# First expert unsplit and taken in one tile per batch, four more experts with unsplit first products

## Chip, cores and metric

One core of one Trainium2 chip. The time is the device time of one execution, in microseconds. A change of about 1% is what a measurement of this kernel can tell from none.

## The reference, cut to what matters

Three stages on 1536 tokens (2 batches of 768), 512 features:

```
attention, 8 heads of 64, masked to keys of the same cluster       -> x[b, s, 512]
for b, s in order:                       # 8 experts, 512 -> 1024 -> 512
    fresh = argmax(x[b,s] @ w_gate)
    e = fresh if s == 0 or sigmoid(x[b,s] @ w_local) < 0.5 else prev_e;  prev_e = e
    p = softmax(x[b,s] @ w_gate)[e]
    out[b,s] = p * (relu(x[b,s] @ w1[e]) @ w2[e])
y = (sigmoid(causal 5-tap conv of out) * (out @ w_val)) @ w_out
```

Each token goes to one expert, which is known only after its batch's attention: the choice is carried along the sequence. Counted from the reference on the inputs it draws (seed 0), the experts 0 to 7 get 54, 88, 118, 164, 82, 73, 71, 118 tokens of batch 0 and 88, 65, 62, 6, 81, 155, 140, 171 of batch 1.

## The kernel before

**Order.** The instructions of each engine stand in the order in which the program writes them, and each engine and DMA queue works its list in that order. Attention runs as 96 items (`for i in range(NI)`, lines 783 to 834); work for later stages is hung on chosen values of `i`. Routing (`route_steps`, lines 496 to 607) is done for half a batch at a time. Its fourth part needs the last item, and so stands alone between the stages: this stretch is the routing gap here. A token's row is scattered to a slot of its expert in `xslots` (`scatter`, line 611, on the POOL queue), and an expert reads its rows from there.

**Experts.** Positions `k` = 0 to 7 take experts in an order given by `AT` (0: expert 0, 1: expert 3, 6: expert 2, 7: expert 1; the four others by their counts). `CAPS` is the number of slots at each position. `HALVED` names experts with one tile for each batch; here experts 1 and 2, 128 slots each. Tokens beyond the slots go to an overflow loop after the last first products (lines 1170 to 1214), which is skipped if there are none. `do_mm1` (line 1045) makes the first products of an expert, 8 groups of 128 hidden features, with the tokens as columns; `do_mm2` (line 1119) the second, with 512 columns. Order: mm1(0), mm1(1), mm2(0), mm1(2), mm2(1), ..., mm1(7), then the halves of positions 6 and 7 (`do_half`, line 1137).

**Precision.** Operands are split in a high part in fp32r and the rest: `w_split` (line 331) copies a weight tile's half to `whi` on ACT and subtracts on DVE to `wlo`. Each product is three fp32r matmuls (line 1063 for the first products, lines 1100 to 1102 for the second). If the last tile of an expert has at most 64 rows, high and rest of its hidden values stand in one stationary operand (`FOLD`, lines 1095 to 1099) and two matmuls do. A weight tile is 1 MB, four to an expert; it lands in a staging buffer (three: `stg`) and is split into one of four pairs of buffers (`ring`).

**Fill-in work.** `tick` (line 967) stands after each group of products and pops one or two entries of `work` (splits, with the DMA of the next raw tile after the second half), two steps of `late` (the overflow plan), and one step, sometimes two, of `conv` (lines 237 to 290: 66 steps that turn the last stage's double-precision weights into two parts on DVE, ACT and POOL, in a buffer that the last stage then uses for its input). A tile of matmuls of fixed length (`keep_warm` and `spin4`, lines 852 to 859) runs in the routing gap, and its output is not used.

Of the kernel before, what the change touches and what calls it, by code (L numbers as in the profile page):

```python
# [8 lines left out]
F32 = mybir.dt.float32  # L9
# [13 lines left out]
CAPS = (192, 192, 300, 240, 224, 184, 256, 256)  # L23
PACK = 64
AT = {0: 0, 1: 3, E - 2: 2, E - 1: 1}
HALVED = (1, 2)
# [13 lines left out]
def routed_attention_moe_kernel(  # L40
# [27 lines left out]
    xin_p = apool("xin", 1)  # L68
    xx_p = apool("xx", 1)
# [27 lines left out]
    cd = cst.tile([128, 4, 32], F32, name="cd")  # L97
    cent_sb = cst.tile([128, 4, 64], F32, name="cent_sb")
# [28 lines left out]
    def const_iota(name, shape, pattern, base, mult=0):  # L127
        t = cst.tile(shape, F32, name=name)
# [3 lines left out]
    wts = const_iota("wts", [128, 24, NC_], [[0, 24], [-1, NC_]], NC_)  # L132
# [27 lines left out]
    wgl_sb = cst.tile([128, 4, 146], F32, name="wgl_sb")  # L160
# [23 lines left out]
    csq = cst.tile([128, 4, 64], F32, name="csq")  # L184
# [26 lines left out]
    worder = []  # L211
    for k in range(E):
        worder += [(k, 0), (k, 1)]
        if k:
            worder += [(k - 1, 2), (k - 1, 3)]
    worder += [(E - 1, 2), (E - 1, 3), (E, 0), (E, 1)]
    wpos = {k: j for j, k in enumerate(worder)}
    whd = dram.tile([2, 128, 2048], F32, name="whd")
# [89 lines left out]
    def ring(j):  # L308
        return rings[0] if j % R == 0 else rings[1]
# [3 lines left out]
    turn = dict(AT)  # L313

    def w_dma(j, q=None):
        k, i = worder[j]
        if k == E:
            W[worder[j]] = [
                p.tile([128, 2048], F32R, tag=g, name=n)
                for p, g, n in (((stg[1], "w", "whi"), (stg[2], "w", "wlo")), ((ring0, "hi", "whi"), (ring0, "lo", "wlo")))[i]  # L320
            ]
            nc.sync.dma_start(W[worder[j]][0].bitcast(F32), whd[i])
            nc.sync.dma_start(W[worder[j]][1].bitcast(F32), wld[i])
            return
        t = wraw[j] = stg[(j + 2) % len(stg)].tile([128, 2048], F32, tag="w", name="wraw")
        if k in AT:
            (q or nc.sync).dma_start(t, wq[4 * AT[k] + i])
        else:
            nc.sync.dma_start(t, wq[bass.ds(turn[k] * 4 + i, 1)].rearrange("o p f -> (o p) f"))

    def w_split(j, half, lo_eng=None):
        if worder[j][0] == E:
            return
# [7 lines left out]
        c = slice(1024 * half, 1024 * half + 1024)  # L341
        t = wraw[j]
        nc.scalar.copy(hi[:, c], t[:, c])  # L343
        (lo_eng or nc.vector).tensor_tensor(lo[:, c], t[:, c], hi[:, c].bitcast(F32), op=ALU.subtract)  # L344
# [425 lines left out]

    for grp in prep_steps(0):
        for f in grp:
            f()
# [9 lines left out]
    for i in range(NI):  # L783
# [53 lines left out]
    last_PV(2)  # L837
    for t in range(3):
        last_logits(t)
    att.close()  # L840
    stg[:] = [wstg, pool("wstg1"), pool("wstg2")]
    w_dma(2)
# [4 lines left out]
    for n, f in enumerate(route_steps(3)):  # L847
        if n == 1:
            last_rows()
        f()  # L850
# [3 lines left out]
    for w in (128, 192, 224, 256):  # L854
        for _ in range(8):
            nc.tensor.matmul(spin4[:, :w], onesr[:, :128], onesr[:, :w], start=True, stop=True)
    for w in (128, 192, 288):
        for _ in range(6):
            nc.tensor.matmul(spin4[:, :w], onesr[:, :128], onesr[:, w:2 * w] if w < 256 else onesr[:, :w], start=True, stop=True)


# [23 lines left out]
    def overflow_steps():  # L885
# [13 lines left out]
            lambda: [v.memset(cape[:, e:e + 1], float(128 if e in HALVED else CAPS[k])) for k, e in AT.items()],  # L899
            lambda: v.memset(cape[:, E:], 128.0),  # L900
# [36 lines left out]

    aps.close()


    xs_p = mpool("xs", 1)
    xt_p = mpool("xt", 1)
    h_p = mpool("hp", 1)
    y_p = mpool("yp", 3)
    mps = ExitStack()
    qpool = lambda name, bufs=1: mps.enter_context(tc.tile_pool(name=name, bufs=bufs, space=PSUM))
# [5 lines left out]
    def queue_w(j):  # L952
        j += R
        if j > LAST:
            return
        work.append(lambda: w_split(j, 0))
        work.append(lambda: (w_split(j, 1), w_next(j)))

    def w_next(j, q=None):
        if j + len(stg) <= LAST:  # L960
            w_dma(j + len(stg), q)
# [21 lines left out]
    FOLD = [0 < (c - 1) % 128 < PACK and n > 1 for c, n in zip(CAPS, NT)]  # L983
# [3 lines left out]
    WX = (max(CAPS[0::2]), max(CAPS[1::2]))  # L987

    XS = {}

    def load_x(k):
# [3 lines left out]
        XS[k] = xs_p.tile([128, -(-WX[k % 2] // 128), XC], F32, tag=f"xs{k % 2}", name="xs")  # L995
        if AT.get(k) in HALVED:
            for t, c in enumerate((AT[k], E + HALVED.index(AT[k]))):
                nc.sync.dma_start(XS[k][:, t, :], xslots[c * SLOT:c * SLOT + 128, :])
# [11 lines left out]
    def do_x(k, part=0):  # L1010
# [6 lines left out]
        if part == 0:  # L1017
# [4 lines left out]
            for ts, r in same:  # L1022
# [3 lines left out]
                xt_p.tile([128, 4, WX[k % 2]], F32R, tag=f"x{s}{k % 2}", name=f"x{s}") for s in ("hi", "lo")  # L1026
            ]
        hi, lo = XT[k]
# [9 lines left out]
        for a, c in qs:  # L1038
            nc.scalar.copy(hi[:, c, :w], xp[:, a, :w])  # L1039
        for a, c in qs:  # L1040
# [439 lines left out]
```

## Time and profile before

| | |
|---|---|
| median of 3 runs (lowest, highest) | 548.25 us (547.82, 551.88) |
| the profiled execution, and its span | 548.82 us, 547.1 us |
| busy share of the span: PE, DVE, ACT, POOL | 96%, 72%, 61%, 20% |
| attention and three parts of routing | to 262 us |
| routing gap | 262 to 280 us |
| experts | 280 to 470 us |
| last stage | 470 to 547 us |

A busy PE is not PE at its peak: matmuls are pipelined, so what a matmul costs is read from the distance between starts, not from its duration. An fp32 matmul shows as two records, an fp32r one as one.

### The profile page before, as it was taken

The numbers are of one execution on the slowest core, as the hardware profiler recorded it, in microseconds if no ns is written. First come the engines' busy times: TensorE is split into PE (matmuls) and PEld (weight loads), VectorE is DVE, ScalarE is ACT, GpSimd is POOL, SyncE is SP. The second block draws the span as 40 slices with busy tenths as digits, with TensorE's granted clock in tenths as the row PEclk, the third lists the DMA queues.
The fourth block names the chain that finished last, engine by engine and source line by source line (L and its number), as shares of the span: only waits on it lengthen the run. The fifth ranks groups of instructions, "written<-read, shape, count | busy, mean of one in ns | idle before, by whom it ended". The sixth has DMA issues, their size and how long they took to land. (4 is left out here: it accounts for less than half of the span.)

```text
span 547.1 us, 9226 instructions
## 1 busy us (share of the span) xinstructions
PE 525.0 (96%) x3361; PEld 421.3 (77%) x3362; DVE 395.2 (72%) x720; ACT 334.6 (61%) x616; POOL 110.8 (20%) x109
## 2 busy tenths in 40 slices
PE   7898999999999999999799999999999999999996
PEld 3675767777677767767489798889889888899885
DVE  5585757575677867645727999979896993499970
ACT  3596868677777778675224665547465664285642
POOL 5011002020204030030400051444535244100000
PEclk9899999999999999999799999999999999999999
DMA  6867697878786757401747867787977677550023
GB/s 141 224 136 227 140 282 193 242 225 225 248 209 222 159 204 155 140 12 68 243 165 272 284 230 242 248 298 236 298 274 263 214 280 256 185 220 1 21 96 115
DMA packets 35205, 107.96 MB, mean 197 GB/s; under 512 B 4753, under 2 KB 5265, under 8 KB 30548
## 3 DMA queue, kind: packets, MB, share of 16 engines
q1 hardware_dynamic: 31700, 98.35, 59.0%
q0 software_dynamic: 2496, 8.40, 4.0%
q10 hardware_dynamic: 960, 0.58, 0.3%
q8 instruction: 27, 0.44, 0.3%
q14 instruction: 22, 0.18, 0.1%
HBM read 58.57 MB, written 29.13 MB: 160 GB/s over the span
## 5 line engine op out<-in xcount | busy, mean ns | idle before, releaser
L653 DVE TENSOR_REDUCE mx<-s 128x1 f32<-128x768 f32 x96 | 91.6, 955 | 59.3 <-PE s L646 51.5
L682 ACT COPY pt<-tp 128x384 f32<-128x384 f32 x148 | 65.7, 484 | 55.1 <-PE tp L677 55.0
L662 ACT ACTIVATE pexp<-s,mx 128x768 f32<-128x768 f32 x96 | 87.2, 908 | 6.6 <-DVE mx L653 4.6
L344 DVE TENSOR_TENSOR wlo<-wraw,whi 128x1024 fp32r<-128x1024 f32 x62 | 84.7, 1381 | 3.8 <-ACT whi L343 3.7
L677 PE MATMUL tp<-ident,pexp 128*128 128x128 f32 x576 | 81.2, 277 | 0.3 <-DVE pt L680 0.2
L677 PEld LDWEIGHTS tp<-ident,pexp 128*128 128x128 f32 x576 | 68.2, 142 | 7.7 <-ACT pt L682 3.4
L343 ACT CAST whi<-wraw 128x1024 fp32r<-128x1024 f32 x64 | 64.9, 1045 | 10.3 <-DMA wraw<-in_wq_dram 10.3
L689 PE MATMUL pv<-pt,vt 128*64 128x384 f32 x360 | 67.8, 498 | 0.1
L642 PE MATMUL s<-st 128*128 128x384 f32 x188 | 57.4, 387 | 1.5 <-ACT pexp L662 1.5
L646 PE MATMUL s<-st 80*128 80x384 f32 x188 | 48.9, 341 | 1.4 <-DMA st<-ohr 1.4
L1101 PE MATMUL yp<-wlo,h 128*128 128x512 f32 (+3 forms) x104 | 41.4, 398 | 1.6 <-DVE wlo L344 1.1
L642 PEld LDWEIGHTS s<-st 128*128 128x128 f32 x188 | 28.6, 191 | 18.4 <-issue 6.7
L1100 PE MATMUL yp<-whi,h 128*128 128x512 f32 (+3 forms) x104 | 41.1, 395 | 0.8 <-PEq L1170 0.8
L1071 ACT ACTIVATE h<-hps 128x384 fp32r<-128x384 f32 (+5 forms) x36 | 18.5, 514 | 38.2 <-PE hps L1066 38.1
L1066 PE MATMUL hps<-xhi,whi 128*128 128x192 f32 (+5 forms) x256 | 41.1, 282 | 0.6 <-ACT xhi L1039 0.6
L1102 PE MATMUL yp<-whi,h 128*128 128x512 f32 (+3 forms) x104 | 41.0, 394 | 0.0
L689 PEld LDWEIGHTS pv<-pt,vt 128*64 128x64 f32 x360 | 21.9, 136 | 24.1 <-issue 23.7
L1066 PE MATMUL hps<-xlo,whi 128*128 128x192 f32 (+5 forms) x256 | 40.4, 279 | 0.0
L1066 PE MATMUL hps<-xhi,wlo 128*128 128x192 f32 (+5 forms) x256 | 40.3, 280 | 0.0
L362 POOL TENSOR_TENSOR xx<-xkq,xx 128x768 fp32r<-128x768 f32 x8 | 14.6, 1819 | 117.9 <-ACT xx L356 117.9
L1066 PEld LDWEIGHTS hps<-xhi,whi 128*128 128x128 f32 x256 | 34.9, 190 | 1.7 <-ACT xhi L1039 0.8
L646 PEld LDWEIGHTS s<-st 80*128 80x128 f32 x188 | 34.5, 190 | 1.7 <-issue 1.7
(269 smaller groups left out, 953.2 us busy)
## 6 DMA issues: line engine op xcount, KB each, us to landing
wraw<-in_wq_dram SPq DMA_DIRECT2D x30, 1024.0 KB, 7.1
st<-xx SPq DMA_DIRECT2D x48, 384.0 KB, 6.1
xslots<-padrow SPq DMA_DIRECT2D x14, 771.0 KB, 11.0
xkq<-in_kq_dram SPq DMA_DIRECT2D x15, 384.0 KB, 5.1
wspace<-in_wd_dram SPq DMA_DIRECT2D x8, 512.0 KB, 6.2
xall<-xnat SPq DMA_DIRECT2D x4, 771.0 KB
vt<-in_v_dram SPq DMA_DIRECT2D x8, 384.0 KB, 3.4
out_dram<-os SPq DMA_DIRECT2D x11, 256.0 KB, 2.0
```

The lines of the kernel that those rows point to most:

```text
L343: nc.scalar.copy(hi[:, c], t[:, c])
L344: (lo_eng or nc.vector).tensor_tensor(lo[:, c], t[:, c], hi[:, c].bitcast(F32), op=ALU.subtract)
L642: nc.tensor.matmul(ps[:, n, :384], st[:, 1, q0:q0 + 128], st[:, 0, 384 * n:384 * n + 384], start=True, stop=False)
L646: nc.tensor.matmul(ps[:, n, :384], st[0:80, 2, q0:q0 + 128], st[0:80, 3, 384 * n:384 * n + 384], start=False, stop=True)
L653: nc.vector.tensor_reduce(mx, ps[:, :, :384], axis=AX.XY, op=ALU.max, negate=True)
L662: nc.scalar.activation(pt, ps[:, :, :384], AF.Exp, bias=mx[:, 0:1], accum_out=Zt[i // 6][:, t, h:h + 1])
L677: nc.tensor.transpose(tp[:, k, :], p[:, 128 * kt:128 * kt + 128], ident)
L682: nc.scalar.copy(dst, tp)
L689: nc.tensor.matmul(PVs[u][64 * h:64 * h + 64, :], Vt[g][:, kt, h, :], PT[u, h][:, kt, :], start=(kt == 0), stop=(kt == NQT - 1), skip_grou ...
L1066: nc.tensor.matmul(hp, a[:, d, fs], c[:, d, :w], start=(n + d == 0), stop=(n + d == 5))
L1100: nc.tensor.matmul(yp[:r], h[:, fa, hi], whv[:, f, :], start=(q == 0 and f == 0), stop=False)
L1101: nc.tensor.matmul(yp[:r], h[:, fa, hi], wlv[:, f, :], start=False, stop=False)
```

## The change

Expert 0 has a tile for each batch now (`HALVED` = 0, 1, 2), 128 slots each, so there are 11 slot ranges in place of 10. Its weights stay fp32 and unsplit, in all four tiles, and so do its tokens and hidden values: one fp32 matmul in place of three fp32r ones. The tile of batch 0 is read in item 84 (`early_load`), transposed in item 89 (`early_rows`), and its first products are placed between the steps of the fourth part of routing, where the unused matmuls were; its second products follow, with the transposes of batch 1's tile before the last one. Then mm1(0), mm2(0), mm1(1), mm1(2), mm2(1) and so on.

Positions 1, 5, 6, 7 take unsplit fp32 first products (`WHOLE`); their second products stay split. Slots: position 1 192 to 176, 5 184 to 176, 6 and 7 256 to 192 (expert 2 as 128 and 64, which is folded; expert 1 as 96 and 96). An unsplit tile goes by DMA straight to its ring buffer once the tile before it there is used; the staging buffers hold only split tiles, in order of need (`pending`). The ring slot that shares `ring0` is now the last of four.

```diff
-CAPS = (192, 192, 300, 240, 224, 184, 256, 256)
+CAPS = (128, 176, 300, 240, 224, 176, 192, 192)
+WHOLE = (0, 1, 5, 6, 7)
-HALVED = (1, 2)
+HALVED = (0, 1, 2)
+ROWS = {0: (128, 128), 1: (96, 96), 2: (128, 64)}
...
+    def early_load():
+        EA["xs"] = xin_p.tile([128, 2, S], F32, tag="x", name="exs")[:, 0, :XC]
+        nc.sync.dma_start(EA["xs"], xslots[0:128, :])
...
+        for d in range(4):
+            nc.tensor.transpose(xp[:, 128 * d:128 * d + 128], xs[:, 128 * d:128 * d + 128], ident)
+        EA["x"] = xx_p.tile([128, 4, S], F32, tag="xx", name="exx")[:, 0, :512]
+        nc.scalar.copy(EA["x"], xp)
...
         if i == 82:
-            w_dma(0)
-        if i in (84, 88):
-            w_split(0, (i - 84) // 4, nc.gpsimd)
+            w_whole(0, ring0)
+        if i == 86:
+            w_whole(1, ring0, "lo")
         if i == 90:
-            w_dma(1)
+            w_whole(2, wstg, "w")
+        if i == 84:
+            early_load()
+        if i == 89:
+            early_rows()
...
-    w_dma(2)
+    w_whole(3, stg[1], "w")
...
-    keep_warm(ps_t.tile([128, 512], F32, tag="t", name="spin3"), 10)
-    spin4 = ps_t.tile([128, 512], F32, tag="t", name="spin4")
...
+    def early_products():
+        x = EA["x"].rearrange("p (d c) -> p d c", d=4)
+        for q in range(2):
+            wv = W[0, q].rearrange("p (d f) -> p d f", d=4)
+            for f in range(4):
+                for d in range(4):
+                    yield nc.tensor.matmul(
+                        eh[:, q, 128 * f:128 * f + 128], wv[:, d, 128 * f:128 * f + 128], x[:, d, :],
+                        start=(d == 0), stop=(d == 3), skip_group_check=True,
+                    )
...
+    r1()
+    last_rows()
+    early(9)
+    r2p()
+    r2d()
+    r3()
+    early(6)
+    r3p()
+    r4()
+    early(3)
+    r4p()
+    r4d()
+    r5()
+    early(32)
+    for q in range(2):
+        for c in range(2):
+            early_relu(q, c)
...
+        if k in WHOLE:
+            (a, c), (a2, c2) = qs
             nc.scalar.copy(hi[:, c, :w], xp[:, a, :w])
+            nc.vector.tensor_copy(hi[:, c2, :w], xp[:, a2, :w])
...
+            if k in WHOLE:
+                terms = [(W[k, q].rearrange("p (d f) -> p d f", d=4), xs[0])]
+            else:
+                whv, wlv = [t.rearrange("p (d f) -> p d f", d=4) for t in W[k, q]]
+                terms = [(whv, xs[0]), (whv, xs[1]), (wlv, xs[0])]
...
+            if k == 0:
+                nc.tensor.matmul(yp[:r], h[:, fa, hi], whv[:, f, :], start=(q == 0 and f == 0), stop=(q == 1 and f == 3))
+                continue
...
     load_x(0)
     load_x(1)
+    w_whole(R, ring1)
+    w_whole(R + 1, ring1)
     for n, k in enumerate(free):
         turn[k] = nc.sync.value_load(ordi[0:1, n:n + 1], min_val=NF, max_val=E - 1)
-    nc.gpsimd.tensor_copy(gate[:TR[1][1], 2:3], XS[1][:TR[1][1], 1, 513:514])
-    w_dma(3, nc.gpsimd)
-    w_split(1, 0)
-    w_split(1, 1)
-    w_next(1, nc.gpsimd)
-    for j in range(2, R):
-        work.append(lambda j=j: w_split(j, 0))
-        work.append(lambda j=j: (w_split(j, 1), w_next(j)))
-    do_x(0)
-    work.insert(2, lambda: keep_rows(3))
+    w_stage(stg[2])
+    queue_split(R + 2)
+    ey = ps_y.tile([128, 512], F32, tag="y", name="ey")
+    for q in range(2):
+        wv = mm2_weights(0, q)[0]
+        for f in range(4):
+            fa = 4 * q + f
+            if fa == 7:
+                do_x(0)
+            nc.tensor.matmul(ey, ehh[:, fa, :], wv[:, f, :], start=(fa == 0), stop=(fa == 7))
+    y = y_p.tile([128, 512], F32, tag="y", name="ysb")
+    nc.scalar.activation(y, ey, AF.Copy, scale=EA["pw"])
+    scatter(x2d, EA["ids"], y, 2 * S, "rows of different tokens")
+    work += [lambda: None, lambda: None, lambda: keep_rows(3)]
     late += overflow_steps()
     do_mm1(0)
     XS["ready"] = True
-    for k in range(1, E - 1):
+    do_mm2(0)
+    do_mm1(1)
+    for k in range(2, E - 1):
         do_mm1(k)
         do_mm2(k - 1)
```

## Rows read from the trace of the kernel before

**Rows 1.** Windows: start:end, length; busy time and (instructions) of PE, PEld, DVE, ACT, POOL; clock; DMA share; GB/s.
```profile
280.41:305.96 25.55, 24.76 (x213) 23.78 (x213) 17.23 (x54) 11.37 (x18) 1.34 (x3) 1.00 0.77 272
305.96:329.32 23.36, 23.36 (x147) 21.61 (x145) 23.12 (x48) 14.91 (x23) 7.08 (x5) 1.00 0.69 238
...
445.73:470.57 24.84, 23.22 (x102) 18.42 (x101) 10.84 (x14) 9.85 (x14) 7.70 (x6) 1.00 0.70 235
```

**Rows 2.** Waits of PE after 262 us: what waited, for what, total, times, longest.
```profile
PE yp L1101 <- DVE wlo L344: 1.1, 2, 0.7
...
PE xp L1034 <- DVE xlo L1041: 0.8, 1, 0.8
```

**Rows 3.** Timeline of PE, routing gap: start, length, line, work, count, [idle before].
```profile
261.85 1.01 PE L754 MATMUL po<-wgl_sb,ut 128*128 128x146 f32 x6
264.82 0.49 PE L530 MATMUL rps<-ident,rr 128*1 128x128 f32 x3 [1.96 <-DVE rr L521]
266.58 0.48 PE L542 MATMUL rps<-ident,sc 1*128 1x1 f32 x3 [1.27 <-DVE sc L534]
...
267.72 4.43 PE L112 MATMUL spin<-onesb 128*128 128x512 bf16 x10
...
278.78 1.02 PE L1034 MATMUL xp<-ident,xs 128*128 128x128 f32 x8 [0.56 <-DMA xs<-xslots]
280.41 0.85 PE L1066 MATMUL hps<-xhi,whi 128*128 128x192 f32 x4 [0.61 <-ACT xhi L1039]
```

**Rows 4.** Timeline of the SP queue: the first experts' token rows are asked for.
```profile
275.72 2.10 SPq L1006 DMA_DIRECT2D xs<-xslots  x4
```

**Rows 5.** Timeline of PE in attention: the only fp32 products with 128 stationary columns.
```profile
222.97 1.01 PE L714 MATMUL po<-wgl_sb,ut 128*128 128x146 f32 x6
223.72 0.61 PE L642 MATMUL s<-st 128*128 128x384 f32 x2
...
251.82 0.91 PE L714 MATMUL po<-wgl_sb,ut 128*128 128x146 f32 x6
252.66 1.53 PE L739 MATMUL pv<-pt,vt 128*64 128x128 f32 x24
```

**Rows 6.** Timeline of PE among the experts: split products in fp32r, three widths.
```profile
282.16 0.61 PE L1066 MATMUL hps<-xhi,whi 128*128 128x192 f32 x4
282.61 0.61 PE L1066 MATMUL hps<-xhi,wlo 128*128 128x192 f32 x4
...
436.13 0.64 PE L1066 MATMUL hps<-xlo,whi 128*128 128x256 f32 x4
436.61 0.63 PE L1066 MATMUL hps<-xhi,wlo 128*128 128x256 f32 x4
...
451.62 0.40 PE L1101 MATMUL yp<-wlo,h 128*128 128x512 f32 x1
451.85 0.39 PE L1102 MATMUL yp<-whi,h 128*128 128x512 f32 x1
```

**Rows 7.** Costliest groups of the page: the high half of a weight split on ACT.
```profile
L343 ACT CAST whi<-wraw 128x1024 fp32r<-128x1024 f32 x64 | 64.9, 1045 | 10.3 <-DMA wraw<-in_wq_dram 10.3
```

**Rows 8.** Windows, columns as in Rows 1: two weight tiles in flight.
```profile
284.00:290.00 6.00, 6.00 (x55) 5.77 (x55) 4.75 (x19) 3.40 (x6) 0.00 (x0) 1.00 0.79 330
```

**Rows 9.** Timeline of POOL, end of the experts: conversion, then the first halves' scatters.
```profile
455.61 2.15 POOL L265 TENSOR_TENSOR wspace<-wspace 128x512 f32<-128x512 f32 x1 [10.44 <-ACT wspace L261]
...
460.54 1.03 POOL L613 DMA_INDIRECT x2d<-ysb,ids  x1 [0.16 <-issue]
```

**Rows 10.** Chain that ended last, end of the experts: start, length, what.
```profile
461.87 4.07 DMA x2d<-ysb,ids
...
466.38 4.15 DMA x2nat<-x2d
```

**Rows 11.** Windows, columns as in Rows 1: the clock in the routing gap.
```profile
262.00:268.00 6.00, 2.47 (x21) 1.73 (x22) 4.29 (x21) 2.51 (x5) 2.40 (x3) 0.82 0.98 298
268.00:274.00 6.00, 6.00 (x26) 3.61 (x25) 4.38 (x17) 0.00 (x0) 2.94 (x3) 0.61 0.61 238
```

More of the change, by code (lines that the diff above doesn't have):

```diff
@@ L208, in routed_attention_moe_kernel @@
     nc.vector.tensor_copy(xnat[:, :, 513], tokid)
[L211 to L215, printed above, removed]
+    worder = [(0, 0), (0, 1), (0, 2), (0, 3), (1, 0), (1, 1)]
+    for k in range(2, E):
+        worder += [(k, 0), (k, 1), (k - 1, 2), (k - 1, 3)]
     worder += [(E - 1, 2), (E - 1, 3), (E, 0), (E, 1)]
     wpos = {k: j for j, k in enumerate(worder)}
+    whole = [k == 0 or k in WHOLE and i < 2 for k, i in worder]
     whd = dram.tile([2, 128, 2048], F32, name="whd")
@@ L846, in routed_attention_moe_kernel, with early, early_relu @@
     rings[1] = ring1
[L847 to L850, printed above, removed]
-    keep_warm(ps_t.tile([128, 512], F32, tag="t", name="spin3"), 10)
-    spin4 = ps_t.tile([128, 512], F32, tag="t", name="spin4")
[L854 to L859, printed above, removed]
+    h_p = mpool("hp", 1)
+    WX = (max(CAPS[0::2]), max(CAPS[1::2]))
+    ehh = h_p.tile([128, 8, 2 * WX[1]], F32, tag="h1", name="ehh")[:, :, :128]
+    def early_products():
[8 more added lines that the diff above has]
+                    )
+    ep = early_products()
+    def early(n):
+        for _ in range(n):
+            next(ep, None)
+    def early_relu(q, c):
+        hp = eh[:, q, 256 * c:256 * c + 256].rearrange("p (f n) -> p f n", f=2)
+        nc.scalar.activation(ehh[:, 4 * q + 2 * c:4 * q + 2 * c + 2], hp, AF.Relu)
+    r1, r2p, r2d, r3, r3p, r4, r4p, r4d, r5 = route_steps(3)
+    r1()
[15 more added lines that the diff above has]
+            early_relu(q, c)
     lt_p = mpool("lt", 1)
@@ L955, in queue_w, with queue_split @@
             return
+        if whole[j]:
+            w_whole(j, ring(j))
+        else:
+            queue_split(j)
+    def queue_split(j):
         work.append(lambda: w_split(j, 0))
[L957 to L961, printed above, removed]
+        work.append(lambda: (w_split(j, 1), w_stage(home[j])))
     conv = convert_steps(wide.tile([128, 12, XC], F32, tag="xn", name="wspace"))
@@ L982, in routed_attention_moe_kernel @@
     NT = [-(-c // 128) for c in CAPS]
-    FOLD = [0 < (c - 1) % 128 < PACK and n > 1 for c, n in zip(CAPS, NT)]
+    FOLD = [
+        ROWS[AT[k]][1] == PACK if k and AT.get(k) in HALVED else 0 < (c - 1) % 128 < PACK and n > 1
+        for k, (c, n) in enumerate(zip(CAPS, NT))
+    ]
     TR = [
@@ L1025, in do_x @@
             XT[k] = [
-                xt_p.tile([128, 4, WX[k % 2]], F32R, tag=f"x{s}{k % 2}", name=f"x{s}") for s in ("hi", "lo")
+                xt_p.tile([128, 4, WX[k % 2]], F32 if k in WHOLE else F32R, tag=f"x{s}{k % 2}", name=f"x{s}")
+                for s in ("hi", "lo")[:1 if k in WHOLE else 2]
             ]
-        hi, lo = XT[k]
+        hi = XT[k][0]
         xp = ps_x.tile([128, 1024], F32, tag="x", name="xp").rearrange("p (d c) -> p d c", d=4 // parts)
@@ L1062, in do_mm1 @@
                     hp = hps[fi][:, 0, :w] if w > 256 else hps[0][:, fi, :w]
-                    terms = [(whv, xhi), (whv, xlo), (wlv, xhi)]
-                    for n, (a, c) in enumerate(terms if k else terms[::2] + terms[1:2]):
+                    for n, (a, c) in enumerate(terms):
                         for d in range(4):
-                            nc.tensor.matmul(hp, a[:, d, fs], c[:, d, :w], start=(n + d == 0), stop=(n + d == 5))
+                            nc.tensor.matmul(
+                                hp, a[:, d, fs], c[:, d, :w], start=(n + d == 0), stop=(n + d == len(terms) + 2)
+                            )
                 m = 2 // len(hps)
@@ L1115, in mm2_weights @@
     def mm2_weights(k, q):
-        whi, wlo = W[k, 2 + q]
-        return whi.rearrange("p (f d) -> p f d", f=4), wlo.rearrange("p (f d) -> p f d", f=4)
+        parts = W[k, 2 + q] if k else [W[0, 2 + q]] * 2
+        return [t.rearrange("p (f d) -> p f d", f=4) for t in parts]
     def do_mm2(k):
@@ L1131, in do_mm2 @@
                     tick()
-            queue_w(wpos[k, 2 + q])
+            if k:
+                queue_w(wpos[k, 2 + q])
+            else:
+                w_stage(stg[q])
         HT.pop(k)
```

125 lines of the change are left out of this document (78 added, 47 removed).

## The prediction, made before the changed kernel was run

> **What bounds the kernel now.** I read the windows by stage first. Among the experts PE is busy 24.76 of 25.55 us in the first stretch and all of the second [rows 1]; the waits of PE there are small [rows 2]. So the matmul stream sets the time of this stage, and a change is worth what it takes out of that stream, where the other engines keep up. DVE is the one to fear: 23.12 of 23.36 us in the second stretch [rows 1]. Then the timeline of the routing gap: PE has nothing that matters between the last logits at 261.85 and the transposes at 278.78; at 267.72 the unused matmuls begin [rows 3]. What ends the gap is the chain routing, scatter, load: the rows are asked for at 275.72 [rows 4]. So work that is put into the gap is free as long as it delays neither the routing steps nor the first transposes. Last the end of the experts: the last stage starts when the first halves' scatter has landed and been read back [rows 10], not when PE is done: PE is busy 23.22 of 24.84 us there [rows 1].
>
> **The price of a matmul.** Split: four matmuls of 192 columns take 282.61 - 282.16 = 0.45 us, so 0.1117 each; of 256 columns 0.48, with the rounding of longer stretches 0.118; of 512 columns 0.23, 0.2315 over longer stretches [rows 6]. From 192 to 256 columns the price hardly moves. Unsplit fp32: three matmuls of 146 columns, six records, take 0.75 us to the next matmul's start in one place and 0.84 in another, 0.125 or 0.140 a record [rows 5]. At 2.4 GHz, 2 x 146 columns take 0.1217: a record streams its columns twice, plus 0.003 to 0.018. I take the middle, 0.0105, and a floor of 0.1117 for 128 columns, since even 192 split columns cost that. A record then costs 0.117 at 128 columns (0.112 to 0.125), 0.157 at 176 (0.150 to 0.165), 0.170 at 192 (0.163 to 0.178), and 0.437 at 512 (0.430 to 0.445); a product is two records. No fp32 row is wider than 146 with 128 stationary columns, so 512 is extrapolated. So unsplit against split, for one product: 0.234 against 0.335 at 128, 0.314 against 0.335 at 176, 0.340 against 0.354 (256 columns before) at 192. Only expert 0 gains much.
>
> The Trainium skill says the same in other terms: true fp32 is four passes through the array ("FP8 and Floating Point Precision", TensorE Precision Notes), and a warm pass costs its columns plus about 2.5 ns ("TensorE: Matmul & The Clock Gate", Part 1). That is an estimate of 0.223, 0.303, 0.330 and 0.863 for the four products; the terms of PE below would sum to 1.7 us less. The row at 0.84 speaks against it, the row at 0.75 for it.
>
> **The change part by part**, against the profiled 548.82 us.
>
> 1. *Attention*, +0.45 (0.3 to 1.0). Four more transposes, about 0.13 each (eight in 1.02 [rows 3], with one start-up), on a full PE. One ACT copy comes, two casts of 1.045 [rows 7] and two subtractions on POOL go; the two small DVE copies wait for a load asked for five items earlier. DMAs: three weight tiles here in place of two, at the end of attention, where nothing else is asked for; one more slot fill on SP.
>
> 2. *Routing gap*, +0.3 (0 to 1.6). Nine products, 18 x 0.117 = 2.1 us, stand ahead of the step at 264.82; from the end of the logits (three products after 261.85, 262.7) they end at 264.8. Six take 1.4, where the next pause is 1.27; three take 0.7, where it is shorter. Each delays the chain by a tenth or two. The 14 left, 3.3 us, end near 271.8 with the shift of part 1. Seven of the second products (7 x 0.87 = 6.1) end near 278, before the rows land near 279.5; the eighth covers the copies after the transposes. So mm1(0) starts near 281.1, where it was 280.41. If the relus or the fourth weight tile were late, the slack of 1.5 us pays first.
>
> 3. *Expert 0*, -5.5 (-5.9 to -4.8). Before: 96 x 0.1117 = 10.72 and, folded, 40 x 0.2315 = 9.26. Now on the path, batch 1's tile alone: 64 x 0.117 = 7.5 and 16 x 0.437 = 7.0.
>
> 4. *First products of positions 1 and 5*, -1.4 (-2.3 to -0.3): 64 x 0.157 = 10.05 for 10.72, twice.
>
> 5. *First products of 6 and 7*, -0.9 (-1.8 to +0.1): 64 x 0.170 = 10.9 for 96 x 0.118 = 11.33, twice.
>
> 6. *End of the experts*, -2.3 (-3.6 to -0.5). The second half of position 6 is folded: 16 matmuls for 24, 1.85 us. PE was busy 23.22 there, 96 x 0.2315 = 22.2 of it matmuls; 88 matmuls and the same rest are 21.4 of the 24.84 [rows 1]. But the chain decides. There are fewer ticks, and counting them the conversion's last POOL work moves behind the first scatter. POOL had it from 455.61 to 460.5, and both scatters stood behind it [rows 9]. Now, from the end of mm1(7): one half is 24 x 0.2315 = 5.6, with the rest of 1.0 and an eviction shorter than a cast the first scatter stands on POOL at 7.3 for 1.0; the conversion's 4.9 end at 13.2, the other scatter (its half is done at 12.1) at 14.3; it lands 4.07 later and is read back 4.15 later [rows 10]: 22.5. What is late next is this chain, by a microsecond over PE. That is 2.3 less than 24.84.
>
> 7. *Waits of PE between 296 and 446*, -0.5 (-1.5 to 0). Of 64 half-tile splits 24 go, so ACT loses 24 x 1.045 [rows 7] and DVE as many subtractions. The waits for `wlo` and `xlo` are 1.9 us [rows 2]; I take a quarter, as the 40 splits left come one a tick through the stretch where DVE is full.
>
> 8. *A new wait on ACT*, +0.5 (0 to +5). Position 2's first raw tile is now asked for behind the token rows and two unsplit tiles, near 278, on SP. Its split stands on ACT between the first and second relu of mm1(0). 3.75 MB at the 330 GB/s of two tiles in flight [rows 8] take 11.4 us, to 289.4. mm2(0) starts near 289.5, and wants the second relu two products later, at 291.3; cast and relu before it take about 1.5. Behind that relu stand the other cast, the copies of the next expert and two relus, all wanted later. So it fits by a few tenths, and the rate decides.
>
> Sum: 0.45 + 0.3 - 5.5 - 1.4 - 0.9 - 2.3 - 0.5 + 0.5 = -9.35, so 539.5 for the profiled execution. The median stands 0.57 lower than that one: 539.0. Ends of all terms: -14.8 and +2.1.
>
> **Rivals.**
>
> *The raw tile is late.* If three tiles and the rows move at the 272 GB/s of the whole first stretch [rows 1], they land at 292, and mm2(0) waits 2 to 3 us; with the other DMAs of this time between them, 6 to 8. Then 541.5 to 547. For it: all of this is now on one queue and ACT works in order. Against: DMA was busy 0.79 of the time at 330 GB/s, not full [rows 8]. Chance 0.13.
>
> *Unsplit first products gain nothing off expert 0.* With 0.018 a record, parts 4 and 5 give -0.2, and if DVE, full in the second stretch, takes the rest, 541.5 to 543. Chance 0.10.
>
> *Slower: the clock falls in the gap.* In the gap the granted clock was 0.82 and then 0.61 of full in two stretches of 6 us [rows 11]: at half for some 7 us, after PE had been busy 2.47 of 6 us. If it falls there now, and the fp32 products with their small pauses don't bring it back, the second early products and mm1(0) take 7 and 7.5 us more: -9.35 + 14.5 = +5, 554 and more. It decides once it lasts beyond the gap. Against: PE would now pause hardly at all, and the granted clock was full in the first stretch, with its transposes and waits [rows 1]. Chance 0.03. The Trainium skill bears on it ("TensorE: Matmul & The Clock Gate", Part 4): transposes don't count as PE activity for the clock. By that rule, the transposes before mm1(0) are a pause; the full clock that the trace shows in the first stretch, which has transposes in it, speaks for no harm.
>
> *Slower: a token too many.* The slots are now near the counts: 62 for 64 (expert 2, batch 1), 170 for 176, 163 for 176, 211 for 224. By the counts no expert overflows, before or after. If one did, the loop would load 4 MB with nothing beside it (13 us at 330 GB/s) and compute for some 15: 565 to 570. Chance 0.02.
>
> **How the numbers follow.** The forecast, 0.70: 535 to 542.8, 539.0 likeliest. The rest of the chance (0.02) is for what I have not seen. A measurement of this kernel tells about 1% from no change, so faster is below 542.8. Faster: 0.70, with 0.05 of the late tile and 0.05 of the second rival: 0.80. Same: 0.15. Slower: 0.05. The range leaves out the clock and the overflow, and the best ends all together: 534.5 to 545.5.
>
> **What would show it.** Starts of two-record products at 128 and 512 columns (parts 2, 3), mm1(0) starting within a microsecond of 281 and mm1(1) near 296, with no wait of PE at mm2(0) (part 8). Positions 1 and 5 near 10 us, 6 and 7 near 10.9. The first transposes of the last stage 22 to 23 us after the end of mm1(7), released by the read-back. Wrong: a clock below 1.00 after 280, a wait of PE for a relu at mm2(0), or an overflow loop in the trace.

## The result, and the profile after

The changed kernel takes 540.33 us (median of 5 runs, 539.74 to 541.24) against 548.25 for the kernel before (5 runs beside it, 547.82 to 551.88). The ratio is 0.9844, with a 95% interval of 0.9809 to 0.988, so it is faster by 1.2 to 1.9%. The prediction said 539.0, within 534.5 to 545.5. The number is near, but behind it two errors of about 8 us each nearly cancel: a wait that was not foreseen, and gains that were larger (2.5 us of them scatter between executions).

The profiled execution took 539.74 us (span 538.1). The two spans are 9.0 us apart. Starts on TensorE cut them into six stretches:

| stretch, by starts on PE | before | after | change | predicted |
|---|---|---|---|---|
| start to the last logits | 261.85 | 259.77 | -2.1 | +0.45 |
| to the first products of position 0 | 18.56 | 18.41 | -0.15 | +0.3 |
| to the first products of position 2 | 34.84 | 35.69 | +0.85 | -5.7 |
| to the second products of position 6 | 131.32 | 126.21 | -5.1 | -2.1 |
| to the first transposes of the last stage | 22.99 | 20.47 | -2.5 | -2.3 |
| to the end | 77.54 | 77.55 | 0 | 0 |

The fourth column is the profile's, the last is the prediction's terms put into these stretches (-0.7 of part 4 in each of the two expert stretches). The third stretch is the miss: the first products of positions 0 and 1 and the second of 0 were to get 5.7 us shorter, and got 0.85 longer.

The timeline of PE after the change, from the gap to the last stage (columns as in [rows 3]):

```profile
260.62 2.17 PE L902 MATMUL eh<-exx,wone 128*128 128x128 f32 x18
...
266.00 3.37 PE L902 MATMUL eh<-exx,wone 128*128 128x128 f32 x28
269.92 6.28 PE L1257 MATMUL ey<-wone,ehh 128*128 128x512 f32 x14 [0.54 <-ACT ehh L915]
276.85 0.63 PE L1118 MATMUL xp<-ident,xs 128*128 128x128 f32 x4 [0.66 <-DMA xs<-xslots]
...
282.62 3.84 PE L1155 MATMUL hps<-xhi,wone 128*128 128x128 f32 x32
286.30 7.22 PE L1188 MATMUL yp<-wone,h 128*128 128x512 f32 x16
293.36 4.94 PE L1155 MATMUL hps<-xhi,wone 128*128 128x176 f32 x32
...
299.04 2.65 PE L1155 MATMUL hps<-xhi,wone 128*128 128x176 f32 x16
308.54 1.45 PE L1118 MATMUL xp<-ident,xs 128*128 128x128 f32 x6 [6.85 <-DVE xlo L1129]
309.92 4.24 PE L1155 MATMUL hps<-xhi,wone 128*128 128x176 f32 x16
...
428.71 10.56 PE L1155 MATMUL hps<-xhi,wone 128*128 128x192 f32 x64
440.08 0.47 PE L1195 MATMUL yp<-whi,h 128*128 128x512 f32 x1 [0.81 <-ACT h L1162]
...
460.55 1.47 PE L1377 MATMUL x2p<-ident,x2nat 128*128 128x128 f32 x12
```

The gap now holds expert 0's first tile, and the waits in it are a few tenths. At 308.54 stands what the prediction did not have: PE waits 6.85 us, in the middle of position 1's first products, for a transpose buffer that is free once VectorE has subtracted the low parts (`xlo`) of the tokens of position 2. Behind it sixteen records take 4.24 us, where sixteen alike took 2.65 before it. The granted clock says why (windows of the changed kernel, columns as in [rows 1]):

```profile
274.00:280.00 6.00, 5.34 (x29) 3.27 (x28) 0.64 (x3) 1.06 (x2) 0.17 (x1) 1.00 0.79 272
...
306.00:310.00 4.00, 1.46 (x7) 1.08 (x7) 4.00 (x16) 1.05 (x1) 0.00 (x0) 0.54 1.01 424
310.00:314.00 4.00, 4.00 (x17) 4.00 (x18) 2.20 (x6) 0.66 (x1) 0.00 (x0) 0.60 0.98 348
```

In the gap, where [rows 11] showed 0.82 and 0.61, the clock is now full (1.00 in the 6 us before these, too). After the long wait it is 0.54 and 0.60, that is 1.2 GHz for part of the stretch. The wait and this cost 6.85 + 1.6 = 8.4 us.

The list of PE's waits from 255 to 470 us in the changed kernel (columns as in [rows 2]) has nothing else of this size, and the waits on `wlo` are gone from it:

```profile
PE xp L1118 <- DVE xlo L1129: 6.9, 1, 6.9
...
PE yp L1195 <- ACT h L1162: 0.8, 1, 0.8
```

Why is the low part late? First VectorE's timeline in the changed kernel, then the SP queue's (start, length, line, work):

```profile
304.58 0.43 DVE L230 TENSOR_SCALAR wspace<-wspace 128x512 int32<-128x512 int32 x1 [4.14 <-DMA wspace<-in_wd_dram]
...
307.02 0.42 DVE L233 TENSOR_SCALAR wspace<-wspace 128x512 int32<-128x512 int32 x1
...
307.72 0.76 DVE L1129 TENSOR_TENSOR xlo<-xp,xhi 128x600 fp32r<-128x600 f32 x1
```

```profile
279.24 11.41 SPq L326 DMA_DIRECT2D wraw<-in_wq_dram  x2
290.94 1.69 SPq L1089 DMA_DIRECT2D xs<-xslots  x3
292.68 0.58 SPq L514 DMA_DIRECT2D xall<-xnat  x1
301.00 0.36 SPq L260 DMA_DIRECT2D wspace<-in_wd_dram  x1
```

Read from the bottom. `wspace`, the conversion's buffer, is the buffer that held the tokens' rows `xnat`, so its load at 301.00 waits until the copy asked at 292.68 is done (SP stands 7.4 us there). VectorE has the first conversion steps (lines 230 to 233) ahead of `xlo`, and stands 4.14 us at the first. In the kernel before, the copy was asked as late, at 292.60, and the load at 299.22; but there `xlo` stood ahead of the first conversion step (VectorE's timeline of the kernel before):

```profile
301.56 0.77 DVE L1041 TENSOR_TENSOR xlo<-xp,xhi 128x600 fp32r<-128x600 f32 x1
...
305.27 0.43 DVE L226 TENSOR_SCALAR wspace<-wspace 128x512 int32<-128x512 int32 x1 [0.67 <-DMA wspace<-in_wd_dram]
```

The change puts the second products of position 0, with their ticks, between the first products of positions 0 and 1, where they stood behind both. So the conversion, which starts after the first products of position 0, is popped earlier than position 2's tokens.

ScalarE's timeline has the raw tile that part 8 feared (changed kernel):

```profile
286.72 1.05 ACT L360 CAST whi<-wraw 128x1024 fp32r<-128x1024 f32 x1 [6.17 <-DMA wraw<-in_wq_dram]
287.67 0.38 ACT L1162 ACTIVATE h<-hps 128x256 f32<-128x256 f32 x1
```

The relu ends at 288.05. The second products start at 286.30 and want it with their third, four records of 0.429 later, at 288.02. It all but fits: to the next work the sixteen records take 7.06 us, against 6.87 in the kernel with the tile second (below), where it lands earlier. So the wait is 0.2 us.

The end of the experts, POOL's timeline in the changed kernel, answers to [rows 9]:

```profile
446.91 1.01 POOL L635 DMA_INDIRECT x2d<-ysb,ids  x1 [7.87 <-ACT ysb L1203]
448.98 1.29 POOL L269 TENSOR_TENSOR wspace<-wspace 128x512 f32<-128x512 f32 x1 [1.06 <-ACT wspace L265]
...
453.04 0.95 POOL L635 DMA_INDIRECT x2d<-ysb,ids  x1 [0.16 <-issue]
```

The order is the predicted one: first scatter, conversion, second scatter. The page's group for the high halves has 40 casts where [rows 7] had 64:

```profile
L360 ACT CAST whi<-wraw 128x1024 fp32r<-128x1024 f32 x40 | 40.7, 1046 | 31.8 <-DMA wraw<-in_wq_dram 16.8
```

### The profile page after: what moved, and what is told of

Read it like the earlier page. It is cut to its first block, busy times and chain, and to the rows that moved or that the text cites. A ratio compares the mean times of both kernels' runs of the same rounds, so it can differ in the third digit from the quotient of the medians.

```text
span 538.1 us, 8817 instructions
## 1 busy us (share of the span) xinstructions
PE 515.7 (96%) x3189; PEld 409.4 (76%) x3190; DVE 353.1 (66%) x693; ACT 310.0 (58%) x592; POOL 91.3 (17%) x106
## 4 chain that ended last, share of the span: by engine, by line
PE 41%; DMA 5%; SPq 1%; DVE 1%; ACT 1%; issue 1%; ACTq 0%; DVEq 0%
PE hps L1155 13%; PE yp L1195 4%; PE yp L1197 4%; PE yp L1196 4%; PE vp L1421 2%; PE vp L1427 2%; PE vp L1422 2%; PE op L1467 2%; PE op L1466 2%; PE op L1465 2%; DMA xall<-xnat 2%; PE yp L1192 1%; PE yp L1193 1%; DMA wraw<-in_wq_dram 1%; PE xp L1118 1%
## 5 line engine op out<-in xcount | busy, mean ns | idle before, releaser
L366 DVE TENSOR_TENSOR wlo<-wraw,whi 128x1024 fp32r<-128x1024 f32 x40 | 52.9, 1330 | 29.6 <-ACT whi L360 29.6
L360 ACT CAST whi<-wraw 128x1024 fp32r<-128x1024 f32 x40 | 40.7, 1046 | 31.8 <-DMA wraw<-in_wq_dram 16.8
L1155 PE MATMUL hps<-xhi,wone 128*128 128x192 f32 (+2 forms) x320 | 50.7, 318 | 0.0
L1155 PEld LDWEIGHTS hps<-xhi,wone 128*128 128x128 f32 x320 | 49.0, 195 | 1.6 <-ACT xhi L1124 0.6
L1162 ACT ACTIVATE h<-hps 128x352 fp32r<-128x352 f32 (+5 forms) x36 | 16.9, 474 | 33.8 <-PE hps L1155 33.7
L1195 PE MATMUL yp<-whi,h 128*112 128x512 f32 (+4 forms) x88 | 35.0, 397 | 0.8 <-ACT h L1162 0.8
L1197 PE MATMUL yp<-whi,h 128*112 128x512 f32 (+4 forms) x88 | 34.7, 394 | 0.0
L1196 PE MATMUL yp<-wlo,h 128*112 128x512 f32 (+4 forms) x88 | 34.7, 394 | 0.0
L1407 DVE SCALAR_TENSOR_TENSOR gt<-xf,convw_sb,gt 128x768 f32<-128x768 f32 x32 | 32.0, 1015 | 0.4
L1165 DVE SCALAR_TENSOR_TENSOR h<-hps,h 128x128 fp32r<-128x128 f32 (+7 forms) x52 | 18.4, 391 | 16.7 <-ACT h L1162 15.1
```

Source lines behind the costliest of these rows:

```text
L366: nc.vector.tensor_tensor(lo[:, c], t[:, c], hi[:, c].bitcast(F32), op=ALU.subtract)
L1155: nc.tensor.matmul(hp, a[:, d, fs], c[:, d, :w], start=(n + d == 0), stop=(n + d == len(terms) + 2))
L1195: nc.tensor.matmul(yp[:r], h[:, fa, hi], whv[:, f, :], start=(q == 0 and f == 0), stop=False)
L1196: nc.tensor.matmul(yp[:r], h[:, fa, hi], wlv[:, f, :], start=False, stop=False)
L1197: nc.tensor.matmul(yp[:r], h[:, fa, lo], whv[:, f, :], start=False, stop=(q == 1 and f == 3))
```

## The experiments

**Is it the late copy?** The first two kernels move the copy of the tokens' rows, out of the fill-in work to the queue's list in the gap: behind the load of position 2's raw tile, or ahead of it.

```diff
     w_stage(stg[2])
+    keep_rows(3)                # first kernel; the second has it ahead of w_stage
...
-    work += [lambda: None, lambda: None, lambda: keep_rows(3)]
+    work += [lambda: None] * 3
```

> The copy of the last routed rows to the overflow buffer is asked for right behind the first raw tile of position 2, before that tile's buffer blocks the SP queue, and not in the ticks of mm2(0). Theory: PE's 6.9 us wait in mm1(1) comes from the conversion's first DVE step, which waits for its load, which waits for this copy; it goes, and with it the half clock behind it: 531.5 to 533.5, no wait of PE over 1.5 us between 280 and 440, clock 1.00 there. Rival: DVE is late in mm1(1) because of the raw tiles and ACT's order; then the wait stays or moves, 539 to 541.

Measured: 537.07 us (536.31 to 538.2), ratio 0.9794 (0.9759 to 0.983). The lines of PE:

```profile
291.18 5.42 PE L1188 MATMUL yp<-wone,h 128*128 128x512 f32 x12 [1.76 <-ACT h L1162]
...
307.29 0.89 PE L1118 MATMUL xp<-ident,xs 128*128 128x128 f32 x6 [2.66 <-DVE xlo L1129]
308.12 2.65 PE L1155 MATMUL hps<-xhi,wone 128*128 128x176 f32 x16
```

The wait on `xlo` falls from 6.85 to 2.66, and the sixteen records behind it are at 2.65 again: the copy's lateness was most of it. What is left is VectorE's order, and a new wait of 1.76 on the relu, since the copy now shares the queues with the raw tile. So the expectation was too good by 3.5 us.

> As the first, but the copy stands ahead of the raw tile. Theory of the raw tile (term 8 of the prediction): 0.77 MB at about 400 GB/s push it 1.9 us later, its cast on ACT holds the second relu of mm1(0) back, and PE waits 1 to 2 us at mm2(0): 1 to 2 us slower than the first. Rival: the raw tile has more slack than that; then no wait at mm2(0) and the same time as the first within 0.5.

Measured: 540.65 us (538.95 to 542.52), ratio 0.9853 (0.9816 to 0.9891), no better than the change itself and 3.6 us slower than the first, where 1 to 2 were expected. The lines of PE:

```profile
293.31 8.43 PE L1188 MATMUL yp<-wone,h 128*128 128x512 f32 x12 [4.31 <-ACT h L1162]
...
311.45 0.89 PE L1118 MATMUL xp<-ident,xs 128*128 128x128 f32 x6 [1.68 <-DVE xlo L1129]
312.27 4.33 PE L1155 MATMUL hps<-xhi,wone 128*128 128x176 f32 x16
```

With the copy's 0.8 MB (384 rows of 2 KB) ahead of it the raw tile makes the second products wait 4.31 us, and the twelve records take 8.43 for 5.42. Behind the wait on `xlo`, here only 1.68, sixteen records take 4.33 for 2.65. The late raw tile is the mechanism of part 8 and of the first rival (a wait of 2 to 3 us, or of 6 to 8), only with a cause that the change does not have.

**Which parts carry the gain?** One kernel keeps expert 0 and position 1 unsplit, with all the new slots, and splits positions 5, 6, 7 again. The other is the kernel before with only the shorter slots of positions 1, 5, 6, 7.

```diff
-WHOLE = (0, 1, 5, 6, 7)
+WHOLE = (0, 1)
```

> The changed kernel with the first products of positions 5, 6 and 7 split again, same slots. Theory (a record costs 0.1487 at 176 and 0.1627 at 192 columns): +1.2 for position 5, +0.3 each for 6 and 7, and 0 to 1 for twelve more half-tile splits on ACT and DVE: 542 to 543.5. Rival (unsplit first products gain nothing off expert 0): 540 to 541.

Measured: 545.3 us (12 runs, 543.07 to 547.24), ratio 0.9936 (0.9909 to 0.9962): the three unsplit positions are worth about 5 us, more than expected, and against -1.6 in parts 4 and 5 for them. From the logits to the second products of position 6 the profiled execution loses 2.1 us on the change's (1.8 of it from the first products of position 2 on, what the expectation has for the records), at the end 0.7, in the last stage 1.5; another 1.2 stand ahead of the last logits, where the kernels do not differ. So half of what the splits can have cost lies outside the stream of products: with 52 half-tile splits in place of 40, a pair of them stands on VectorE at 441.34 for 5.30 us (3.09 in the change), and the conversion and the read-back are late behind it (PE waits 1.2 us for the read-back).

```diff
-CAPS = (192, 192, 300, 240, 224, 184, 256, 256)
+CAPS = (192, 176, 300, 240, 224, 176, 192, 192)
+ROWS = {1: (96, 96), 2: (128, 64)}
```

> The kernel before with the slots of the change at positions 1, 5, 6 and 7, everything split and expert 0 as before. Theory: first products of 6 and 7 from 256 to 192 columns, 0.6 us each; the folded second half of position 6, 1.85 to 3.2 at the end of the experts: 543.5 to 545.5. Rival: the chain scatter, read back sets the end and the folded half gains nothing: 546.5 to 547.5.

Measured: 550.46 us (12 runs, 544.54 to 551.8), ratio 1.0015 (0.9984 to 1.0047): no gain, where some 4 us were expected. PE and ACT show where it went:

```profile
450.25 0.59 PE L1105 MATMUL yp<-wlo,h 128*128 128x512 f32 x1 [4.77 <-issue]
```

```profile
449.47 1.99 ACT L344 CAST whi<-wraw 128x1024 fp32r<-128x1024 f32 x2 [4.49 <-DMA wraw<-in_wq_dram]
```

From the logits to the second products of position 6 it wins 2.0 us; then the last raw tile, of position 7, has not landed, PE waits 4.77 us for its halves and goes on at a lower clock (0.68 from 445 to 452, 0.81 from 452 to 458), and the end is 4.2 us longer than before. Shorter products bring PE sooner to a tile that comes no sooner. In the change, where the first products of positions 6 and 7 need no split, this wait does not appear.

**Can the rest of the wait go?** From here the copy stays early. The raw tile of position 2 is asked ahead of the slots' rows, in the queue's idle time (the numbers of the experts' tiles are read into registers ahead of it, for it needs one); in a second kernel the copy goes there too.

```diff
+    w_stage(stg[2])             # and keep_rows(3), in the second kernel
     load_x(0)
     load_x(1)
     w_whole(R, ring1)
     w_whole(R + 1, ring1)
+    keep_rows(3)                # first kernel
...
-    w_stage(stg[2])
```

> The changed kernel with the raw tile of position 2 asked ahead of the loads of the slots' rows, in the queue's idle time of the gap, and the copy of the tokens' rows right behind the loads of the gap. Theory (the queue of SP, blocked by the last raw tile, makes the copy late, the copy makes the conversion's load late, and VectorE, in order, holds the conversion's first step ahead of the tokens' low parts of position 2): the copy lands at about 286, the first products of position 1 wait at most 1.5 us on the low parts (6.85 in the changed kernel, 2.7 in the kernel with the copy right behind the tile's load), and the second products of position 0 wait on no relu; 531.5 to 534. Rival A: the early megabyte competes with the rows of the slots, the first products of position 0 start a microsecond or more later, 535 to 537. Rival B: the wait stays near 2.7 because VectorE's steps ahead of the low parts set it, not the load; 534 to 536.

Measured: 535.63 us (534.36 to 537.43), ratio 0.9764 (0.9725 to 0.9804). No wait at the second products and 1.66 on `xlo`, near the 1.5 that the theory allowed; but also the wait of its rival A, ahead of the transposes of position 0 (PE's timeline):

```profile
279.03 0.63 PE L1118 MATMUL xp<-ident,xs 128*128 128x128 f32 x4 [2.47 <-DMA xs<-xslots]
...
280.57 5.16 PE L1155 MATMUL hps<-xhi,wone 128*128 128x128 f32 x32
```

With the megabyte ahead of them PE waits 2.47 us for the 128 rows of 2 KB, for 0.66 in the change, and the 32 records behind that wait take 5.16 us for 3.74.

> As the kernel with the raw tile of position 2 in the idle time, but with the copy of the tokens' rows there too, ahead of the loads of the slots' rows. If the queue of SP alone orders these transfers, the same time within 1 us. If transfers that run together slow each other, the rows of the slots come later, and the first products of position 0 start 1 to 4 us later, 533 to 537.

Measured: 540.36 us (539.33 to 543.35), ratio 0.9861 (0.9821 to 0.99). The first entry of PE's waits:

```profile
PE xp L1118 <- DMA xs<-xslots: 6.4, 1, 6.4
```

Later than expected, too (533 to 537). With 1.8 MB ahead PE waits 6.4 us for the rows: the queue has time to spare in the gap, the DMA engines do not (their share is 1.04 from 276 to 282, for 0.79 from 274 to 280 in the change).

**Is it the order on VectorE?** Here only the start of the conversion moves behind the first products of position 1: in the change as it stands, and then in the kernel with the tile in the idle time.

```diff
     do_mm1(0)
-    XS["ready"] = True
     do_mm2(0)
     do_mm1(1)
+    XS["ready"] = True
```

> The changed kernel, in which only the conversion of the last weights begins later, behind the first products of position 1; its copy of the tokens' rows stays late. Theory (the conversion's first step stands ahead of the low parts on VectorE and waits for its load): the wait of 6.85 us goes to at most 1, and with it the stretch at the lower clock behind it; 531.5 to 534. Rival (the low parts are late for a reason of their own, the rows of position 2 or the copy to the high parts): the wait stays at 4 us or more, 538 to 540. Third: the conversion is pushed past the end of the experts and gives 1 to 4 us back there, 534 to 537.

Measured: 540.62 us (539.36 to 543.25), ratio 0.9863 (0.9824 to 0.9902): no better than the change, in sum. PE's timeline says that the theory is right and the time was given back:

```profile
302.04 0.89 PE L1118 MATMUL xp<-ident,xs 128*128 128x128 f32 x6 [0.83 <-DVE xlo L1129]
...
432.58 0.47 PE L1195 MATMUL yp<-whi,h 128*128 128x512 f32 x1 [0.82 <-ACT h L1162]
...
456.65 0.63 PE L1377 MATMUL x2p<-ident,x2nat 128*128 128x128 f32 x4 [3.46 <-DMA x2nat<-x2d]
```

The wait goes from 6.85 to 0.83 with the copy as late as in the change (asked at 292.33), so the order decides, not the copy alone: the wait needs both. (Another 0.9 us on the second `xlo` comes behind it, in the first products of position 2.) The second products of position 6 start at 432.58 for 440.08, but the last stage starts 24.1 us behind them for 20.5, and more is lost to its own waits and clock.

> As the kernel with the raw tile of position 2 in the idle time, and the conversion of the last weights begins only behind the first products of position 1. Theory: no step of the conversion is ahead of the low parts of position 2's tokens on VectorE, so the wait on them goes to at most 0.5 us; 531 to 533. Rival: the conversion then runs past the last first products and lengthens the end of the experts by 1 to 4 us, 533 to 537.

Measured: 541.01 us (539.77 to 542.27), ratio 0.9861 (0.9824 to 0.9899): no wait on `xlo` at all, 4.4 us of waits on the read-back. Its rival had the mechanism; the time is above the rival's 533 to 537 as well.

The next two let the conversion catch up, with a second step at every second or third tick where the code has every fourth (`beats[0] % 4 == 3`).

> The kernel with the later conversion, in which a second step of the conversion now goes with every second tick in place of every fourth, so that it ends about where it does in the changed kernel. Theory (the late conversion removed the wait of 6.85 us on the low parts and gave it back at the end of the experts, as 4.8 us of waits on the read-back and a half clock behind them, because the conversion's buffer is the read-back's and VectorE's and POOL's last steps stand ahead of the last scatters): the read-back's waits fall to at most 1 us, the wait on the low parts stays at most 1.5; 531 to 534. Rival (the loss at the end comes from the experts ending sooner than the read-back can, whatever the conversion does): the waits of 4 us stay, 538 to 541.

> The same with a second step at every third tick: some five steps fewer made up. If the end of the conversion decides, the waits on the read-back lie between those of the two others, 533 to 538; if it does not, the same as the kernel with the later conversion, 538 to 541.

Measured: 537.32 us (535.56 to 539.93), ratio 0.9782 (0.9749 to 0.9815), and 537.76 (536.53 to 538.61), ratio 0.9799 (0.9768 to 0.983). Both better than 540.62, so the end of the conversion does decide; neither gets under 1 us of wait on the read-back (4.5 and 2.8 in all), and the second is no worse than the first. The theory's size was off again.

**The best order.** The raw tile is asked between the rows of position 0 and those of position 1; else as in the kernel with the tile in the idle time. The second of this pair starts the conversion two ticks later.

```diff
     load_x(0)
+    w_stage(stg[2])
     load_x(1)
     w_whole(R, ring1)
     w_whole(R + 1, ring1)
+    keep_rows(3)
...
-    w_stage(stg[2])
```

> The changed kernel with the raw tile of position 2 asked between the two loads of slots' rows, ahead of the 2 MB of unsplit tiles, and the copy of the tokens' rows right behind these. Theory: the rows of position 0 are not delayed (first transposes within 0.5 us of where they stand in the changed kernel, counted from the routing's logits; 2.5 us later in the kernel with the tile ahead of all loads), the relu of position 0 waits for no raw tile, the low parts of position 2 make a wait of at most 2.7; 533 to 535.5. Rival (the megabyte delays whatever stands behind it): the rows of position 1 or the unsplit tiles of position 1 come late, a wait of 1 to 4 us ahead of the first products of position 1, 536 to 540.

Measured: 532.1 us (531.5 to 533.79), ratio 0.9698 (0.9674 to 0.9723), faster than both kernels and than the expected 533 to 535.5: its interval lies under the change's 0.9809 to 0.988. PE's timeline, then SP's:

```profile
277.33 0.63 PE L1118 MATMUL xp<-ident,xs 128*128 128x128 f32 x4
...
286.77 7.03 PE L1188 MATMUL yp<-wone,h 128*128 128x512 f32 x16
293.64 4.94 PE L1155 MATMUL hps<-xhi,wone 128*128 128x176 f32 x32
...
303.50 0.89 PE L1118 MATMUL xp<-ident,xs 128*128 128x128 f32 x6 [1.66 <-DVE xlo L1129]
...
453.34 1.47 PE L1378 MATMUL x2p<-ident,x2nat 128*128 128x128 f32 x12
```

```profile
274.56 0.34 SPq L1077 DMA_DIRECT2D xs<-xslots  x1
275.13 0.35 SPq L326 DMA_DIRECT2D wraw<-in_wq_dram  x1
...
278.11 0.38 SPq L514 DMA_DIRECT2D xall<-xnat  x1
285.03 0.35 SPq L326 DMA_DIRECT2D wraw<-in_wq_dram  x1
```

The rows of position 0 don't wait, the second products run through, and what is left of the 8.4 us is 1.66. From the first products of position 0 to those of position 2 it takes 28.03 us, for 35.69 in the change.

> The same with the conversion of the last weights beginning behind the second products of position 0, two ticks later. If VectorE's order (the conversion's first steps ahead of the low parts) sets the rest of the wait, it falls by 1 to 2 us, 532 to 534.5; if the end of the experts is then bound by the read-back, it comes back there and the time is that of the kernel before it, within 1 us.

Measured: 537.78 us (534.08 to 539.76), ratio 0.9794 (0.976 to 0.9829). The waits of PE:

```profile
PE x2p L1378 <- DMA x2nat<-x2d: 2.8, 2, 2.0
PE hps L1155 <- DVE xlo L1129: 1.7, 1, 1.7
```

The wait on the first `xlo` is gone, so VectorE's order did set it. The conversion's steps now stand ahead of the second `xlo`, for the same 1.7 us, and two ticks come back at the end: 2.1 us up to the last stage and 0.9 in it, not the one allowed for. Put together, twelve kernels with the new order show the end's rule. Both columns count from the start of position 6's second products:

| kernel | last conversion result is written out | last stage starts |
|---|---|---|
| the change; copy behind the tile; copy ahead of it; tile in the idle time; tile and copy there; tile second | 12.8 in each | 20.5 in each |
| positions 5, 6 and 7 split again | 14.9 | 21.2 |
| late, every second tick | 16.7 | 22.5 |
| late, every third tick; tile second and two ticks later | 17.3, 17.3 | 22.5, 22.6 |
| late; tile in the idle time and late | 18.9, 18.9 | 24.1, 24.1 |

The read-back lands in the conversion's buffer, and it is asked 2.4 to 3.4 us after that last write in each of them. It does not wait for a scatter there: in the kernel with two ticks later the second scatter is issued at 445.99, the last write at 450.87, the read-back at 453.32. At 12.8 PE's own work hides this; at 14.9 PE waits 0.5 us for the read-back before its first transposes, and 1.8 to 3.5 at 17 and more.

## Why the prediction was near, and where it failed

**Part 1, attention.** The trace shows -2.1 for the +0.45. It can't be told from scatter: in eleven other profiled executions with the new attention the last logits start between 259.6 and 261.3, and at 260.22 in the kernel with only the slots changed, which has the old one. The profiled execution of before, at 261.85, is the latest of all; a scatter of 2 us hides a term of half a microsecond.

**Part 2, the gap.** Right: -0.15 for +0.3. The early products fit into the routing's pauses, and the first products of position 0 begin 18.41 us after the logits. The rival of the falling clock did not come: 1.00 throughout.

**Parts 3 to 5, prices.** An fp32 record takes 0.1117 at 128 columns (3.57 us for the first 32 of position 0, to the start of the transposes behind them), 0.1487 at 176, 0.1627 at 192 and 0.429 at 512 (the sixteen of the kernel with the tile second, in 6.87 us); 0.117, 0.157, 0.170 and 0.437 were taken, the first three 5% high, the last 2%. At 128 the bound below was the answer: 0.1117, what an fp32r matmul of 192 columns costs too [rows 6]. The estimate from the Trainium skill's pages ("FP8 and Floating Point Precision", TensorE Precision Notes, and "TensorE: Matmul & The Clock Gate", Part 1), 0.223, 0.303, 0.330 and 0.863 a product, stands against 0.223, 0.297, 0.325 and 0.859 measured. It was the better of the two at all four widths, so the row at 0.75 should have had more weight than that at 0.84.

**The step that failed** is part 7, "Waits of PE between 296 and 446, -0.5 (-1.5 to 0)". It allowed for no wait that comes, and in this stretch came one of 6.85, with 1.6 of clock behind it. For the move of position 0's second products ahead of position 1's first products only the raw tile's wait (part 8) was worked out, not the conversion steps that their ticks put ahead of position 2's `xlo`. Two sets of kernels show it: moving the copy takes the wait to 2.66, moving the conversion to 0.83. Without these 8.4 us the change would stand at 531.9 (an estimate: 540.33 less 8.4), and the best kernel, which keeps 1.66 of them, measures 532.1. So the rest of the sum was too small by about 8 us: 2.5 is the scatter of the first stretch, 1.9 the third stretch (about 1 of it the lower prices above and what part 8 did not cost; 0.8 that the first products of positions 0 and 1 took 11.2 and 11.05 us before, where 10.72 was taken for each), 3.0 the middle, and the rest the gap and the end. That the two errors met is luck, and the scatter is a part of it: the medians differ by 7.9 us, the two spans by 9.0. The prediction's own sign of being wrong, a clock below 1.00 after 280, did come.

**Part 8 and the first rival.** The place was right. The cost, +0.5, was 0.2 in the change: the "few tenths" to spare were not there, and not much was missing. The kernel with the copy ahead shows what lies behind the margin: 4.31 us and 3 of clock. What was not seen is that the same blocked queue delays others: SP stood from 279.24 to 290.6 at the second raw tile, with the copy behind it.

**Parts 4, 5 and 7, the middle stretch.** -5.1 for -2.1. Of it 1.1, 1.3 and 0.95 are from the starts of positions 5, 6 and 7's first products to the next work; half of these 3.3 is the forecast, the other half the lower prices. The remaining 1.8 lie in the second products between them, where the waits on `wlo` (1.1) [rows 2] are gone; part 7 had 0.5 for all its waits. The second rival, nothing off expert 0, is refuted by the kernel that splits 5, 6 and 7 again: +5 us. That kernel loses 1.8 us in this stretch, no more than the prices of the records, and the kernel with only the slots wins 2.0 there; the 1.3 left of the 5.1 belong to neither alone, and no run parts them. What the splits cost besides (0.7 at the end and 1.5 in the last stage, when there are 52 of them) is in no term, but from 64 to 40 splits the last stage did not change.

**Part 6.** -2.5 for -2.3, but by another limit. The chain of scatter and read-back was to set 22.5 us after the end of position 7's first products; PE's own work did, at 21.3. In the kernel before, too, the chain cost PE only 0.41 us, behind transposes that did not wait for it (PE's timeline):

```profile
470.57 1.09 PE L1271 MATMUL x2p<-ident,x2nat 128*128 128x128 f32 x8 [0.41 <-DMA x2nat<-x2d]
```

So the eight matmuls less (1.85 us) went straight into the time. The second scatter starts on POOL 13.8 us after that end, near the count (14.3), but the read-back is asked 3.0 later, where 4.07 was taken for the landing [rows 10]. The kernels with the late conversion show the chain where it does decide. **The overflow** did not come.

## What to carry to other kernels

When a block of work moves in a program in which fill-in steps hang on ticks, list for each in-order engine what its fill-in steps now stand in front of, and what these wait for; a step that waits for a load holds everything behind it. A queue's idle time is not the DMA engines': ask small, urgent transfers first, the large ones right behind. A gain in the middle is worth only what the chain at the end allows: measure how late its last input may come, here 12.8 us after a fixed point cost nothing and 14.9 did, before spending it.

## What the runs showed of the hardware

A wait of PE of 2.66 us left the next sixteen records at 2.65 us, the full rate, and one of 2.06 at the edge of the gap left 32 records at 3.74 (granted clock 1.00 in both). After waits of 4.31 and 6.85 us twelve records took 8.43 for 5.42 and sixteen 4.24 for 2.65, at granted clocks of 0.64 and 0.54 to 0.60; after the same wait (6.86) in the kernel that splits 5, 6 and 7 again sixteen took 5.01; and 32 records took 5.16 for 3.74, at 0.64, after a wait of 2.47 at the edge of the gap. So a wait cost up to 3 us beyond its own length, and the length of the last wait alone does not tell it: after one of 1.68, with the one of 4.31 some 18 us ahead of it, sixteen records took 4.33, at 0.70.

An fp32 product with 128 stationary columns cost 0.223 us at 128 columns, 0.297 at 176, 0.325 at 192 and 0.859 at 512; the three fp32r products in its place 0.335 at 192 and 0.694 at 512 [rows 6]. At 512 columns the split is the cheaper on PE.
